# Linear attention into a softplus MLP on one core: x of tiles 9 to 11 turned by VectorE instead of TensorE, o of tiles 15 to 35 scaled by ScalarE head by head instead of by VectorE

## The chip, the cores and the metric

The kernel runs on one core of a Trainium2 chip. The core has TensorE (PE in the profile, with its weight loads as PEld), VectorE (DVE), ScalarE (ACT), GpSimd (POOL) and SyncE (SP, which here issues nearly all DMAs), each with its own in-order queue, an on-chip memory (SBUF) with 128 partitions, and PSUM, eight banks of 128 x 512 fp32 words into which TensorE accumulates. The metric is the device time of one launch in microseconds, lower is better.

## What is computed

The reference has two blocks, in fp32 precision. B, H, S, D are 8, 8, 576, 64.

```python
kv = np.einsum('bhsd,bhse->bhde', k, v)
out = np.einsum('bhsd,bhde->bhse', q, kv)
rms = np.sqrt(np.mean(out * out, axis=-1, keepdims=True) + 1e-06)
attn = out / rms * g_norm
x = attn.transpose(0, 2, 1, 3).reshape(4608, 512)
h = x @ w_in                       # 512 -> 2048
g = np.maximum(h, 0.0) + np.log1p(np.exp(-np.abs(h)))   # softplus
out = g @ w_out                    # 2048 -> 512
```

## The kernel before

**Tiles and blocks.** The 4608 tokens (batch times sequence) are 36 tiles of 128. Three tiles are a block (12 blocks of 384 tokens), four a wide block (9 of 512). `w_in` and `w_out` are cut into 16 chunks of 128 of the 2048 hidden units.

**Precision from three products.** TensorE multiplies a reduced-precision fp32 format (fp32r) at full rate. Each operand is kept as three pieces (a rounded high part, what it leaves, and a combination of both), and three matmuls with them make up one precise product. ScalarE writes the high piece, VectorE the other two. This split happens for x (`split`), for the weights (`split_weight`) and for softplus's output (`low`, `less`).

**Attention.** `kv_of(b)` loads k and v of a batch in five chunks each and sums k^T v in PSUM (L676); ScalarE copies the result out. `rows(t)` makes x of tile t:

- q is turned to q^T, for batches 0 and 1 by TensorE (`turn_q`, L756) with a ScalarE copy (L763), later by VectorE from blocks of 32 (L731, loads at L598);
- `out_rows` (L700) multiplies q^T by kv, 32 small matmuls, into a half of PSUM banks 2 and 3 (ring `o`, two places);
- ScalarE squares (L773), VectorE sums per head (`reduce`, L704), POOL takes the power -1/2 (`root`, L707 and L708), VectorE multiplies o by it (`norm`, L712) into x. `g_norm` is multiplied into `w_in` beforehand;
- x is turned to x^T. For tiles below `BY_PE` TensorE does it (`turn_x`, L718, four transposes); the first `AT_ONCE` = 6 tiles are split at once from PSUM; ScalarE copies x^T out of PSUM (L782) and SP stores it to DRAM (L783). For the other tiles VectorE transposes blocks of 32 x 32 in SBUF (`turn_blocks`, L799), and when the three tiles of a block are done SP stores them with four DMAs (L803), whose access pattern does the rest of the turn. It leaves the tokens of a block in another order, so the output rows of these tiles are put back in place by four DMAs per tile in the last pass (`leave`, L905) where others need one (L910).

From tile 6 on, x^T comes back from DRAM (`x_again`, L821) and is split (L620, L623, L626).

**MLP, first part.** 64 steps (`step`): blocks 0 to 3 go over hidden chunks 0 to 3, blocks 4 to 11 over chunks 0 to 5. A step is 12 matmuls of 384 columns for h (L843), softplus on ScalarE (L865), the split (L867, L854, L858) and 9 matmuls of 512 columns into the output sums (L850).

**MLP, second part.** The other chunks run over the wide blocks, 48 wide steps in two passes (`wide_step`, L1030 for h with a scheme that replaces eight products by seven, L1100 for the output). Partial sums go to DRAM between passes (`leave`, L895 and L910; `enter`, L889).

**Order.** The program order is written by a planner (`Plan.order`) before anything is emitted. Each piece of work is a task with an engine, a cost in ns, inputs, places it takes in rings of buffers, and a position `pos` in units of steps. The planner walks through its own clock: among the tasks of an engine that can start within 150 ns of the earliest, the lowest position goes first. `behind` ties a load to the first matmuls of a step: it may not be issued before them. Rows of tile t may not start before those of tile t - 1 (`follows`). From tile `BY_PE` + 1 on, an odd tile takes the position of the even tile before it and waits for both tiles' inputs, so that the two run together. Where TensorE would stand idle in the plan, a filler matmul of the identity is put in (`warm`, L1181); its result isn't used. Positions come from tables P0 to P7: `CONVERT` and `FETCH` (from P0) place the conversions and loads of the first eight weights, P4 the rows of the 36 tiles, P5 the kv and q of the batches, P7 the first k, v and q loads, P1 and P2 the later weights, P6 the units of x in the wide passes.

```python
        if n == 0: P4[t] + t * EARLY[0] + EARLY[1]
        else:      P4[t] + first_step["block", n] - (EARLY[2] if n == 1 else EARLY[3]) + t % TB * (len(CHUNKS[n]) // TB)
```

That is `x_pos(t)`, the position of tile t's rows, with `EARLY = P0[16:27]`.

Of the kernel before, what the change touches and what calls it, by code (L numbers as in the profile page):

```python
# [12 lines left out]
AF = mybir.ActivationFunctionType  # L13
# [42 lines left out]
class Plan:  # L56
# [20 lines left out]
        return Slot(ring)  # L77

    def add(self, engine, ns, run, after=(), pos=0.0, take=(), give=(), size=0, behind=None, follows=None, kind="all"):
        t = Task(engine, ns, run, [a for a in after if a is not None], pos, list(take), list(give), size)  # L80
        for s in t.give:
            s.readers += 1
        self.tasks.append(t)
        t.follows = follows
        t.behind = behind
        t.kind = kind
        return t
# [113 lines left out]
def kernel(  # L201
# [24 lines left out]
    nc = tc.nc  # L226
    B, H, S, D = q.shape
# [3 lines left out]
    NP = H // 2  # L231
# [14 lines left out]
    STEPS = [(ph, n, p) for ph in (1, 2) for n in range(n_wide) for p in PAIRS[ph - 1][n]]  # L246
    LAST = 2

    P0 = [-45.94, -26.77, -11.8, 0.28, -29.91, -5.64, -2.86, 3.84, -103.4, -98.98, -69.3, -76.66, -68.5, -24.67, -23.22, -34.97, 8.15, -43.02, 7.47, 9.69, 7.18, 18.16, -12.1, 4.75, 1.0, 95.98, -6.45, 6.38, 7.69, 5.17]
    P4 = [-30.17, -6.08, 16.93, -33.9, -22.35, -28.91, -17.33, -7.12, -9.75, -2.59, 0.87, 2.93, -12.14, -3.26, 0.98, 3.76, 7.8, -3.0, -2.25, 7.68, 20.89, 50.27, -0.5, -0.13, 26.66, 22.67, -11.61, -5.55, 2.74, 0.64, -0.48, 1.34, 0.64, 1.68, -8.4, -1.37]  # L250
    P5 = [1.24, -5.69, -2.28, 1.58, 5.58, 0.43, 5.83, -7.56, 3.01, -2.95, 3.18, 1.42, -14.52, 0.57, -1.29, -1.34]
    P6 = [-0.39, 4.6, -0.28, -2.24, -0.01, 1.05, 1.77, -3.9, -2.15, 0.85, 1.85, -1.74, 6.34, -2.44, -0.13, 3.82, 7.89, 0.51]
    P7 = [-23.78, -17.98, -11.85, -14.93, 0.41, 1.61, 7.35, 2.7, -25.02, -6.6, -15.2, -4.48, -2.14, 0.64, 2.93, 0.97, 4.67, 5.36, 3.33, 6.57, -10.37, 2.36, -14.11, -9.89, -7.11, 12.91, -2.89, 14.55, 12.59, 9.35]
    CONVERT, FETCH, EARLY, LATER = P0[:8], P0[8:16], P0[16:27], P0[27:]
    P1 = [48.8, 48.65, 66.31, 74.64, 125.35, 131.27, -11.31, 54.26, 67.75, 469.13, 282.82, 195.86]
    P2 = [22.14, 35.93, 25.02, 37.31, 52.38, 81.67, 74.61, 116.65, 106.27, 111.35, 100.82, -152.23, 99.52, 221.41, 428.54, -173.95, 119.58, -155.43, 317.87, 212.07, -7.69]
    P3 = [3.0, 2.86, 5.84, -16.31, 1.53, 3.03, 3.55, -20.64, 3.15, 2.55, 1.38, 1.52, 1.27, 0.75, 2.42, -1.39]
    SPLIT = {p: (P1[i], P1[6 + i]) for i, p in enumerate((2, 3, 4, 5, 6, 7))}
    TAKEN = {c: (P2[c - 6], P2[4 + c]) for c in range(6, 16)}
    LEAD, APART, AHEAD, MM2, LATE, SPLIT_G = P3[0], P3[1], P3[2], P3[3:11], P3[11:14], P3[14]  # L260
    EARLIER = P3[15]
    PACE = 2.5
    BY_PE = 12
    AT_ONCE = 2 * TB

    ctx.enter_context(tc.manual_schedule())
# [13 lines left out]
    scale = const.tile([P, 1], F32, name="scale")  # L280
# [4 lines left out]
    def space(name, words, late, dtype=F32):  # L285

        if (name, late) not in spaces:
# [13 lines left out]
                 h=2, o=2, tp=1, s0=1, s1=1, s2=1, s3=1, w=15, wh=3, u=4, u1=1, gvp=2, xl=2, ab=2)  # L301
# [9 lines left out]
    slot, add = plan.slot, plan.add  # L311
# [276 lines left out]
    def load_q(b):  # L588


        q_slots[b], q_loads[b] = slot("qa"), []
        pos = x_pos(first_tile[b] + 1) - EARLY[7] + P5[B + b]

# [93 lines left out]
    def rows(t):  # L687
        pos = x_pos(t)
        tp, qT, o, x, r, xp, xg = (slot(n) for n in ("tp", "n", "o", "x", "r", "tp" if t < AT_ONCE else "o", "n"))
# [36 lines left out]
        for b, r0, n, s0 in parts(t):  # L726
# [26 lines left out]
            def turn_q(n=n, q_s=q_s, at_qa=at_qa, tp=slot("tp" if t < AT_ONCE else "o")):  # L753
                y = new(tp, [P, NP, P])
                for p in range(NP):
# [4 lines left out]
                     behind=pos - 3.5, follows=first_load[0] if t and at_qa else None)  # L760
            first_load.append(ld)
            a = add("PE", 440, turn_q, [ld], pos - 1, [tp], [q_s])
# [6 lines left out]
        a = o_task = add("PE", 484, out_rows, turned + need, x_pos(t - second), [o], [qT], kind="rows", follows=rows_done.get(t - 1))  # L769
        rows_done[t] = a  # L770
        for pt in parts(t):
            o_tasks.setdefault(pt[0], []).append(a)
        a = add("ACT", 600, lambda: nc.scalar.activation(new(x, [P, H, D]).rearrange("s (a k) d -> s a (k d)", k=2), o.tile, func=AF.Square,  # L773
                                                              scale=D ** -0.5), [a], pos, [x])
        a = add("DVE", 690, reduce, [a], pos, [r])
        a = add("POOL", 2300, root, [a], pos)
        a = add("DVE", 700, norm, [a, o_task], pos, [], [o, r])
        if t < BY_PE:
            a = add("PE", 440, turn_x, [a], pos + 0.5, [xp], [x])
            if t < AT_ONCE:  # L780
                split(t, xp, a, pos + 0.5)
            a = add("ACT", 600, lambda: nc.scalar.copy(new(xg, [P, KD, P]), xp.tile), [a], pos + 1, [xg], [xp])  # L782
            x_there[t] = [add("SP", 450, lambda: nc.sync.dma_start(  # L783
                out=x_of(t), in_=xg.tile), [a], pos + 1, [], [xg], 1000)]
            return
# [3 lines left out]
        n, i = divmod(t, TB)  # L789
        g = TB if n < n_blocks - 1 else 1  # L790
        i0, i = i - i % g, i % g
        if i == 0:
            xb_slots[n] = slot("xb"), []
        xb, turns = xb_slots[n]
# [8 lines left out]
            nc.sync.dma_start(out=xd[n][:, i0 * P + a * g * BL:i0 * P + (a + 1) * g * BL].rearrange("(b i) m -> i b m", i=BL),  # L803
                              in_=xb.tile[a * BL:(a + 1) * BL].rearrange("i b t j -> i b (t j)"))

        turns.append(add("DVE", 710, turn_blocks, [a], pos, [] if i else [xb], [x], follows=turns[-1] if i else None))
        if i == g - 1:
            stores = [add("SP", 450, lambda a=a: store(a), turns, pos + 0.5, [], [xb], 820 if g > 1 else 490)
                      for a in range(P // BL)]
# [339 lines left out]
    for c in range(KF):  # L1149
        for j in (2 * c, 2 * c + 1):  # L1150
            if c < OWN:
                pos = CONVERT[j] if c < 4 else LATER[c - 4] + LATER[2] * (j % 2)
                weight(j, pos, FETCH[j] if c < 4 else pos, pos - 3.5)
            else:
                fetch, pos = (x + P2[20] * (j % 2) for x in TAKEN[c])
# [61 lines left out]
```

## Time and profile before

| | |
|---|---|
| median of 4 runs | 873.57 us (872.46 to 874.26) |
| the profiled execution | 874.26 us |
| its span, first to last instruction | 872.5 us |
| granted TensorE clock | 0.999 |
| TensorE matmuls, busy | 855.4 us, 98% |
| TensorE weight loads, busy | 758.3 us, 87% |
| VectorE busy | 703.9 us, 81%, 992 instructions |
| ScalarE busy | 521.8 us, 60%, 979 instructions |
| POOL busy | 78.2 us, 9% |
| DMA | 167.07 MB, 191 GB/s in the mean |

In the views below, a row of groups has the line, engine, operation, output and input tiles by the program's names, shapes, count, then busy us and mean ns of one, then the idle time of its engine just before it and what ended it. A row of waits has engine and line that waited, what it waited for, us in total, times, and the longest. Busy TensorE doesn't mean TensorE at its peak rate, and a wait for several things is put down to the one that came last.

### The profile page before, as it was taken

The page shows a single profiled execution, that of the slowest core. Times are in us where ns is not written, and L with a number is a line of the kernel's source. Part 1 is how long each engine was busy: PE and PEld are TensorE (multiplying, and loading weights), DVE is VectorE, ACT ScalarE, POOL GpSimd, SP SyncE. Part 2 cuts the span into 40 slices and gives each one's busy share as a digit, 9 for nine tenths or more (in the row PEclk, how much of TensorE's full clock was granted, in tenths as well). Part 3 has the DMA queues.
Part 4 walks back from the last instruction along what each step waited for, and adds up shares of the span by engine and source line. Part 5 has one row for each costly group of instructions (what it writes and reads, how often), then busy time and mean ns, then how long its engine had stood idle before and what let it go on. Part 6 is the DMA issues. An engine that isn't in the chain of part 4 may idle for free.

```text
span 872.5 us, 17016 instructions
## 1 busy us (share of the span) xinstructions
PE 855.4 (98%) x6464; PEld 758.3 (87%) x6464; DVE 703.9 (81%) x992; ACT 521.8 (60%) x979; POOL 78.2 (9%) x79
## 2 busy tenths in 40 slices
PE   7799999999999999999999999999999999999998
PEld 5578888989898899989988998888899899999986
DVE  7888888978788788798988779877788766878873
ACT  5766654545444567766757556655777555566653
POOL 0352223121112300000000000000000000000000
PEclk9999999999999999999999999999999999999999
DMA  9999999898993765427554545655364753777764
GB/s 265 283 224 221 269 219 251 171 276 211 219 169 104 176 194 174 149 85 250 181 156 147 181 156 187 201 157 180 110 195 135 238 160 107 244 222 237 236 187 130
DMA packets 239634, 167.07 MB, mean 191 GB/s; under 512 B 106304, under 2 KB 198464, under 8 KB 239552
## 3 DMA queue, kind: packets, MB, share of 16 engines
q1 hardware_dynamic: 239392, 165.99, 68.6%
q8 instruction: 50, 0.82, 0.4%
q14 instruction: 32, 0.26, 0.1%
q10 hardware_dynamic: 160, 0.00, 0.0%
HBM read 112.98 MB, written 52.95 MB: 190 GB/s over the span
## 4 chain that ended last, share of the span: by engine, by line
PE 89%; DMA 4%; DVE 2%; SPq 2%; ACT 1%; issue 1%; POOL 0%; DVEq 0%; POOLq 0%; ACTq 0%
PE banks L1100 30%; PE banks L1030 27%; PE banks L850 13%; PE banks L843 13%; PE banks L700 2%; PE banks L676 2%; DMA early<-in_q_dram 2%; SPq L598 1%; DMA loads<-in_v_dram 1%; DMA x<-w 1%; DMA loads<-in_k_dram 1%; SPq L665 1%; DVE units L623 0%; PE banks L1181 0%; DVE half L712 0%
## 5 line engine op out<-in xcount | busy, mean ns | idle before, releaser
L1100 PE MATMUL banks<-pieces,gv 128*128 128x512 f32 x696 | 217.9, 394 | 0.0
L843 PE MATMUL banks<-units,pieces 128*128 128x384 f32 x768 | 145.8, 338 | 0.0
L850 PE MATMUL banks<-pieces,gv 128*128 128x512 f32 x576 | 145.5, 396 | 0.0
L843 PEld LDWEIGHTS banks<-units,pieces 128*128 128x128 f32 x768 | 135.1, 188 | 5.1
L1100 PEld LDWEIGHTS banks<-pieces,gv 128*128 128x128 f32 x696 | 121.2, 189 | 18.1
L1100 PE MATMUL banks<-pieces,g_False 128*128 128x512 f32 x348 | 136.4, 392 | 0.1
L1030 PEld LDWEIGHTS banks<-units,pieces 128*128 128x128 f32 x948 | 126.9, 190 | 8.3 <-ACT banks L1075 1.3
L1030 PE MATMUL banks<-units,pieces 128*128 128x256 f32 x948 | 132.5, 282 | 0.0
L850 PEld LDWEIGHTS banks<-pieces,gv 128*128 128x128 f32 x576 | 106.3, 188 | 20.9
L1090 DVE TENSOR_TENSOR gv<-g_True,gv 128x1024 fp32r<-128x1024 f32 x48 | 58.7, 1224 | 34.0 <-ACT gv L1087 34.0
L865 ACT ACTIVATE half<-banks 128x384 f32<-128x384 f32 x64 | 31.4, 490 | 89.1 <-PE banks L843 88.9
L1100 PEld LDWEIGHTS banks<-pieces,g_False 128*128 128x128 f32 x348 | 65.4, 188 | 15.4 <-DVE g_False L1093 0.6
L708 POOL TENSOR_TENSOR r<-r,half 128x8 f32<-128x8 f32 x36 | 63.2, 1756 | 3.0
L1079 DVE TENSOR_TENSOR g_True<-banks,g_True 128x512 f32<-128x512 f32 x48 | 33.2, 691 | 37.3 <-PE banks L1030 33.3
L1057 ACT ACTIVATE g_True<-banks 128x256 f32<-128x256 f32 x96 | 36.8, 383 | 39.7 <-PE banks L1030 39.2
L1093 DVE SCALAR_TENSOR_TENSOR g_False<-gv 128x1024 fp32r<-128x1024 f32 x48 | 58.7, 1223 | 1.3
L993 DVE TENSOR_TENSOR units<-loads,units 128x1024 fp32r<-128x1024 f32 x42 | 51.2, 1219 | 8.7 <-ACT units L990 8.7
L1030 PEld LDWEIGHTS banks<-units,w 128*128 128x128 f32 x396 | 52.5, 189 | 2.8
L1030 PE MATMUL banks<-units,w 128*128 128x256 f32 x396 | 54.8, 281 | 0.0
L990 ACT ACTIVATE units<-loads 128x1024 fp32r<-128x1024 f32 x42 | 44.5, 1058 | 17.0 <-PE banks L1030 11.0
L996 DVE SCALAR_TENSOR_TENSOR units<-units 128x1024 fp32r<-128x1024 f32 x42 | 51.3, 1223 | 1.6
L1087 ACT ACTIVATE gv<-g_True 128x1024 fp32r<-128x1024 f32 x48 | 51.0, 1061 | 1.5
(116 smaller groups left out, 1295.4 us busy)
## 6 DMA issues: line engine op xcount, KB each, us to landing
loads<-x SPq DMA_DIRECT2D x180, 128.0 KB, 2.8
part<-m SPq DMA_DIRECT2D x72, 256.0 KB, 2.8
m<-part SPq DMA_DIRECT2D x72, 256.0 KB, 3.5
loads<-form SPq DMA_DIRECT2D x45, 256.0 KB, 3.3
form<-loads SPq DMA_DIRECT2D x36, 256.0 KB, 2.7
raw<-in_moe_w_in_dram SPq DMA_DIRECT2D x16, 512.0 KB, 4.6
loads<-in_k_dram SPq DMA_DIRECT2D x32, 256.0 KB, 4.5
loads<-in_v_dram SPq DMA_DIRECT2D x32, 256.0 KB, 4.8
```

What stands on the lines that cost most here:

```text
L708: nc.gpsimd.tensor_tensor(out=r.tile, in0=r.tile, in1=half, op=ALU.pow)
L843: nc.tensor.matmul(hp, lhsT=w_in.tile[:, i, kd * P:(kd + 1) * P], rhs=xv.tile[:, i, kd], start=(m == 0), stop=(m == 3 * KD - 1))
L850: nc.tensor.matmul(mine[i].tile, lhsT=gv.tile[:, m, i * P:(i + 1) * P], rhs=w_out.tile[:, m], start=(c == cs[0] and m == 0), stop=(c == cs ...
L990: nc.scalar.activation(part_of(0, F32R), xl.tile if m > 1 else xl.tile[:, 0], func=AF.Copy, scale=DOWN)
L993: nc.vector.tensor_tensor(out=part_of(1, F32R), in0=xl.tile if m > 1 else xl.tile[:, 0], in1=part_of(0), op=ALU.subtract)
L996: nc.vector.scalar_tensor_tensor(out=part_of(2, F32R), in0=part_of(1), scalar=-RADIX, in1=part_of(0), op0=ALU.mult, op1=ALU.add)
L1030: nc.tensor.matmul(place(q), lhsT=w[:, m, at:at + P], rhs=dst.tile[:, m, v, kd] if u < 6 else dst.tile[:, m, kd], start=(u == 0 and not m ...
L1057: nc.scalar.activation(dst, src, func=AF.Softplus, scale=1.0 + E)
L1087: nc.scalar.activation(gvt(0, F32R), gt(), func=AF.Copy, scale=DOWN)
L1090: nc.vector.tensor_tensor(out=gvt(1, F32R), in0=gt(), in1=gvt(0), op=ALU.subtract)
L1093: nc.vector.scalar_tensor_tensor(out=gt(F32R), in0=gvt(1), scalar=-RADIX, in1=gvt(0), op0=ALU.mult, op1=ALU.add)
L1100: nc.tensor.matmul(mine[i].tile, lhsT=(gvt(m, F32R) if m < 2 else gt(F32R))[:, c, i * P:(i + 1) * P], rhs=outs[c].tile[:, m], start=fresh ...
```

## The change

`BY_PE` goes from 12 to 9: x of tiles 9, 10 and 11 takes VectorE's path (`turn_blocks`, one block of three tiles) instead of `turn_x`, ScalarE's copy and three stores. As `BY_PE` is also used in `second` and in `leave`, tiles 10 and 11 now run together, and the output rows of tiles 9 to 11 are stored with four DMAs per tile.

A new constant `BY_ACT` = 15: from tile 15 on, the multiplication of o by the per-head factor is done by ScalarE, in two tasks of four instructions (`norm_half`), each on the 64 columns of one head with the head's factor as a per-partition scale, in place of one VectorE instruction for all eight heads.

All tables P0 to P7 get other numbers, and positions are rounded to four places.

```diff
--- before.py
+++ after.py
@@ -77,6 +77,7 @@
         return Slot(ring)
 
     def add(self, engine, ns, run, after=(), pos=0.0, take=(), give=(), size=0, behind=None, follows=None, kind="all"):
+        pos, behind = round(pos, 4), None if behind is None else round(behind, 4)
         t = Task(engine, ns, run, [a for a in after if a is not None], pos, list(take), list(give), size)
         for s in t.give:
             s.readers += 1
@@ -246,21 +247,22 @@
     STEPS = [(ph, n, p) for ph in (1, 2) for n in range(n_wide) for p in PAIRS[ph - 1][n]]
     LAST = 2
 
-    P0 = [-45.94, -26.77, -11.8, 0.28, -29.91, -5.64, -2.86, 3.84, -103.4, -98.98, -69.3, -76.66, -68.5, -24.67, -23.22, -34.97, 8.15, -43.02, 7.47, 9.69, 7.18, 18.16, -12.1, 4.75, 1.0, 95.98, -6.45, 6.38, 7.69, 5.17]
-    P4 = [-30.17, -6.08, 16.93, -33.9, -22.35, -28.91, -17.33, -7.12, -9.75, -2.59, 0.87, 2.93, -12.14, -3.26, 0.98, 3.76, 7.8, -3.0, -2.25, 7.68, 20.89, 50.27, -0.5, -0.13, 26.66, 22.67, -11.61, -5.55, 2.74, 0.64, -0.48, 1.34, 0.64, 1.68, -8.4, -1.37]
-    P5 = [1.24, -5.69, -2.28, 1.58, 5.58, 0.43, 5.83, -7.56, 3.01, -2.95, 3.18, 1.42, -14.52, 0.57, -1.29, -1.34]
-    P6 = [-0.39, 4.6, -0.28, -2.24, -0.01, 1.05, 1.77, -3.9, -2.15, 0.85, 1.85, -1.74, 6.34, -2.44, -0.13, 3.82, 7.89, 0.51]
-    P7 = [-23.78, -17.98, -11.85, -14.93, 0.41, 1.61, 7.35, 2.7, -25.02, -6.6, -15.2, -4.48, -2.14, 0.64, 2.93, 0.97, 4.67, 5.36, 3.33, 6.57, -10.37, 2.36, -14.11, -9.89, -7.11, 12.91, -2.89, 14.55, 12.59, 9.35]
+    P0 = [-51.25, -13.31, -28.11, -0.89, -52.51, -4.9, -19.5, 4.49, -140.62, -126.44, -88.51, -96.46, -100.38, -25.43, -13.98, -42.06, -28.49, -36.42, 39.41, 8.82, 7.23, 22.63, -4.14, 5.1, 0.41, 111.95, -26.5, 7.48, 7.3, 9.79]
+    P4 = [-49.82, -17.44, 59.53, -31.74, -18.17, -38.56, -25.79, -19.7, -34.43, 4.73, -0.03, 1.95, -28.04, -3.12, 0.5, 25.22, 41.05, -18.71, -5.41, -2.55, 39.47, 59.13, -19.46, -5.64, 37.83, -4.77, -24.21, -8.59, 4.34, 26.33, -70.4, 7.18, -0.45, 18.64, -3.13, -7.41]
+    P5 = [15.74, 2.22, -4.87, 7.5, 6.25, 15.53, 4.47, -15.68, -3.43, 32.09, 1.42, -2.23, -6.68, 3.2, -5.1, -0.0]
+    P6 = [-5.0, 0.89, -7.05, -17.85, -7.47, -3.43, 4.32, -4.14, -3.37, 0.93, -0.84, -12.54, 1.35, 1.5, 2.03, 6.96, -6.46, 4.89]
+    P7 = [-37.82, -42.49, -14.06, -16.33, 3.68, 6.23, -8.09, 6.34, -35.36, -15.84, -14.25, -22.01, -0.93, 0.05, 24.27, 24.25, 1.0, 14.93, 4.27, 14.15, -7.88, 6.08, -27.64, -8.35, -2.32, 37.25, -1.33, 16.45, 19.25, 23.37]
     CONVERT, FETCH, EARLY, LATER = P0[:8], P0[8:16], P0[16:27], P0[27:]
-    P1 = [48.8, 48.65, 66.31, 74.64, 125.35, 131.27, -11.31, 54.26, 67.75, 469.13, 282.82, 195.86]
-    P2 = [22.14, 35.93, 25.02, 37.31, 52.38, 81.67, 74.61, 116.65, 106.27, 111.35, 100.82, -152.23, 99.52, 221.41, 428.54, -173.95, 119.58, -155.43, 317.87, 212.07, -7.69]
-    P3 = [3.0, 2.86, 5.84, -16.31, 1.53, 3.03, 3.55, -20.64, 3.15, 2.55, 1.38, 1.52, 1.27, 0.75, 2.42, -1.39]
+    P1 = [52.19, 51.92, 57.77, 61.84, 111.12, 131.27, 23.25, 58.31, 66.8, 507.77, 251.61, 203.48]
+    P2 = [23.31, 35.62, 27.15, 38.1, 47.95, 82.07, 69.55, 100.38, 112.9, 104.49, 277.58, -87.75, 236.15, 134.35, 481.42, -149.3, 298.33, -275.07, 382.49, 222.8, -6.08]
+    P3 = [1.73, 2.69, 5.92, -7.65, 1.34, 2.39, 4.99, -16.33, 3.25, 3.38, 3.17, 1.76, 1.0, -5.76, 0.17, -3.08]
     SPLIT = {p: (P1[i], P1[6 + i]) for i, p in enumerate((2, 3, 4, 5, 6, 7))}
     TAKEN = {c: (P2[c - 6], P2[4 + c]) for c in range(6, 16)}
     LEAD, APART, AHEAD, MM2, LATE, SPLIT_G = P3[0], P3[1], P3[2], P3[3:11], P3[11:14], P3[14]
     EARLIER = P3[15]
     PACE = 2.5
-    BY_PE = 12
+    BY_PE = 9
+    BY_ACT = 15
     AT_ONCE = 2 * TB
 
     ctx.enter_context(tc.manual_schedule())
@@ -774,9 +776,17 @@
                                                               scale=D ** -0.5), [a], pos, [x])
         a = add("DVE", 690, reduce, [a], pos, [r])
         a = add("POOL", 2300, root, [a], pos)
-        a = add("DVE", 700, norm, [a, o_task], pos, [], [o, r])
+        def norm_half(e):
+            for h in range(e * NP, e * NP + NP):
+                nc.scalar.activation(x.tile[:, h], o.tile[:, h // 2, h % 2 * D:h % 2 * D + D], func=AF.Identity,
+                                     scale=r.tile[:, h:h + 1])
+
+        if t < BY_ACT:
+            a = [add("DVE", 700, norm, [a, o_task], pos, [], [o, r])]
+        else:
+            a = [add("ACT", 900, lambda e=e: norm_half(e), [a, o_task], pos, [], [o, r]) for e in range(2)]
         if t < BY_PE:
-            a = add("PE", 440, turn_x, [a], pos + 0.5, [xp], [x])
+            a = add("PE", 440, turn_x, a, pos + 0.5, [xp], [x])
             if t < AT_ONCE:
                 split(t, xp, a, pos + 0.5)
             a = add("ACT", 600, lambda: nc.scalar.copy(new(xg, [P, KD, P]), xp.tile), [a], pos + 1, [xg], [xp])
@@ -803,7 +813,7 @@
             nc.sync.dma_start(out=xd[n][:, i0 * P + a * g * BL:i0 * P + (a + 1) * g * BL].rearrange("(b i) m -> i b m", i=BL),
                               in_=xb.tile[a * BL:(a + 1) * BL].rearrange("i b t j -> i b (t j)"))
 
-        turns.append(add("DVE", 710, turn_blocks, [a], pos, [] if i else [xb], [x], follows=turns[-1] if i else None))
+        turns.append(add("DVE", 710, turn_blocks, a, pos, [] if i else [xb], [x], follows=turns[-1] if i else None))
         if i == g - 1:
             stores = [add("SP", 450, lambda a=a: store(a), turns, pos + 0.5, [], [xb], 820 if g > 1 else 490)
                       for a in range(P // BL)]
```

## The prediction

> **What bounds the kernel now.** I read the page's busy shares first, then the chain that ended last, then busy time by stage, then TensorE's waits stage by stage.
>
> ```profile
> PE 855.4 (98%) x6464; PEld 758.3 (87%) x6464; DVE 703.9 (81%) x992; ACT 521.8 (60%) x979; POOL 78.2 (9%) x79
> PE 89%; DMA 4%; DVE 2%; SPq 2%; ACT 1%; issue 1%; POOL 0%; DVEq 0%; POOLq 0%; ACTq 0%
> ```
>
> TensorE (PE) is busy 98% of 872.5 us and carries 89% of the chain. What is left, DMA above all, lies in the first part of the chain. The stages say where TensorE has room (columns: stretch, its length, busy time of PE, PEld, DVE, ACT, POOL, granted clock, DMA share, GB/s):
>
> ```profile
> 40.00:50.00 10.00, 8.93 (x159) 7.31 (x155) 8.51 (x15) 6.03 (x12) 4.12 (x4) 1.00 1.04 238
> 70.00:82.70 12.70, 12.59 (x199) 10.40 (x196) 10.73 (x20) 8.98 (x19) 3.88 (x4) 1.00 1.00 178
> 82.70:123.00 40.30, 38.67 (x406) 33.94 (x404) 35.74 (x61) 23.96 (x47) 10.61 (x10) 1.00 0.99 230
> 123.00:308.00 185.00, 185.00 (x1715) 165.13 (x1712) 154.82 (x266) 89.25 (x177) 43.03 (x41) 1.00 0.85 203
> 363.20:868.60 505.40, 505.26 (x3159) 454.07 (x3157) 397.81 (x466) 313.11 (x572) 0.00 (x0) 1.00 0.57 179
> ```
>
> From 123 us to 868.6 us TensorE doesn't stop. The 48 wide steps fill the last 505.4 us at 10.53 us each (42 matmuls of 256 columns, 24 of 512). Time can be won there only by taking TensorE work away. Between 82.7 and 868 us TensorE's waits consist of one line, and from 61 us on of two:
>
> ```profile
> PE banks L676 <- DMA loads<-in_v_dram: 1.6, 1, 1.6
> PE banks L718 <- DVE half L712: 0.5, 1, 0.5
> ```
>
> Before 82.7 us the stretches add up to 11.4 us of idle TensorE, and all of the fillers (L1181, matmuls whose result nobody reads, issued by the plan where it has nothing else) are there:
>
> ```profile
> L1181 PE MATMUL banks<-ident_r 128*128 128x512 f32 x52 | 18.8, 480 | 2.0 <-DVE ident_r L1141 1.6 <-ACT pieces L509 0.2
> ```
>
> So 30.2 us of the first 82.7 are without useful TensorE work; 8.9 of them pass before the first k and v have landed at 8.88 us, and 21.3 depend on the order of loads and of the first tiles. From 10 us on DMA's share is about 1 there, and DVE is busy 81 to 95%.
>
> **The change part by part.** Rows that price it:
>
> ```profile
> L712 DVE TENSOR_TENSOR half<-banks,r 128x512 f32<-128x512 f32 x36 | 24.7, 687 | 6.7 <-PE banks L700 4.1 <-POOL r L708 2.4
> L799 DVE STREAM_TRANSPOSE turned<-half 128x512 f32<-128x512 f32 x24 | 16.7, 704 | 0.5
> L782 ACT COPY w<-banks 128x512 f32<-128x512 f32 x12 | 7.0, 587 | 4.4 <-PE banks L718 4.4
> L895 ACT ACTIVATE m<-banks,scale 128x512 f32<-128x512 f32 x36 | 24.6, 688 | 15.7 <-PE banks L1100 15.7
> L895 ACT ACTIVATE m<-banks 128x512 f32<-128x512 f32 x72 | 41.7, 594 | 11.9 <-PE banks L1100 6.7 <-PE banks L850 2.3 <-DVE m L444 1.4
> L1071 ACT COPY banks<-banks 128x256 f32<-128x256 f32 x48 | 17.4, 362 | 6.4 <-PE banks L1030 6.3
> ```
>
> Tiles 9 to 11. TensorE loses three groups of four transposes (L718). In the timeline the groups at 80.12, 82.71 and 93.63 us push the next matmul back by 0.42, 0.35 and 0.36 us: 1.1 us of TensorE, in a part where it has no other gap, so I count it in full. ScalarE loses 3 x 0.587 = 1.8 us (L782), VectorE gains 3 x 0.704 = 2.1 us (L799), at 90% busy. Three stores of 256 KB (median 4.8 us to landing) become four of 192 KB (4.0 us), which can only start when the third tile is turned; SP issues one more. These tiles' output stores in the last pass become four DMAs each instead of one: nine more on SP, at 0.42 us 3.8 us, hidden by SP's waits there (the pass's stores and loads wait for ACT and DVE for tens of us). Without that cover, the loads queued behind them (L940) would be late by up to 1.3 us per tile. Tile 11 now shares its place with 10 instead of standing alone, at most one switch, 0.1 us: taken as nothing.
>
> Tiles 15 to 35. VectorE loses 21 x 0.687 = 14.4 us, mostly in 123 to 308 us, where it falls from 84% to about 77%. TensorE waits for it there nowhere, so that is worth nothing by itself. ScalarE gets 168 instructions of 64 columns with a per-row scale, of a shape the trace doesn't show. Row: (587 - 362) / 256 = 0.88 ns a column gives 362 - 192 x 0.88 = 193 ns, and a scale from a tile adds 688 - 594 = 94: 287 ns. Two equal instructions in a row (L773) took 1.09 us instead of 1.19, so some 0.10 us overlaps. Four then take 0.85 us, and 1.15 without overlap; I take 0.9, near the lower end, since back-to-back work of this engine overlaps wherever the timeline shows it. 42 x 0.9 = 38 us (36 to 48) more on ScalarE, which goes from 48% to about 69% in that stretch. A tile's x comes 2 x 0.9 - 0.69 = 1.1 us later, and its part of the o bank is free 1.1 us later; both are hidden as long as the next pair of tiles is some 16 us away, as it is between the L700 groups at 145.64, 161.07 and 185.41 us. If that cover is gone, the next out_rows stands behind a bank for up to 1.1 us a tile.
>
> The Trainium skill, page "ScalarE: Activation LUTs", section "Rules for kernel authors", speaks against this part: multiplies belong on VectorE. From the same page's section "What ACT_TABLE_LOAD costs" one would estimate 186 + 53 + 93 = 332 ns for one such instruction, 93 of them overlapped, 1.05 us for four, and 44 us in all in place of 38; its 93 ns for a scale by pointer agrees with the 94 of the rows. The rule looks at the cost of the instruction; this trace has the idle time on ScalarE to pay for it, and no wait of TensorE that VectorE's shorter list would shorten.
>
> The order. All position tables change. They don't add work, but decide what the first 82.7 us look like. Two effects can be priced. Rows of tile 2, the last tile that step 0 needs, stand at -33.9 instead of -9.8 and so sixth instead of seventh among the tiles; tiles follow each other there by (42.29 - 28.18) / 3 = 4.7 us (starts of L718): up to 4.7 us won. Against that, the last k or v chunk of batch 0 has one more weight (512 KB) and one more q tile (256 KB) in front of it: 768 KB at the 283 to 293 GB/s of 10 to 40 us is 2.7 us lost. Between -4.7 and +2.7 I take -2.0: the chain into the first L843 at 45.85 goes through a tile's split (L623 at 40.31), not through batch 0's loads, whose last lands at 26.4. The wait of 1.6 us at 121.74 is for a v chunk of batch 4; its load goes from position 26.6 to 16.9 and may start one step earlier, its matmuls 1.7 steps earlier. Ends: -1.6 and 0; I take -1.6, as the priority of the load moves much further than the matmul.
>
> Sum against the profiled execution (874.26 us, span 872.5 and 1.8 around it): -1.1 - 1.6 - 2.0 = -4.7, 869.6 us. That execution lies 0.7 above the median of the four; 873.57 - 4.7 = 868.9, so 869.0.
>
> **The rivals.**
>
> *ScalarE's new work holds up softplus (slower).* In a steady step L843 ends at 179.2, softplus (L865) starts at 179.23, L858 ends at 181.53 and its L850 starts at 183.22: 1.6 us of slack. One half (0.9) in front of softplus fits. Two in a row (1.7 to 2.3) don't, and lose 0.1 to 0.7 us; it decides from 1.6 us of foreign work ahead of one softplus. At 21 tiles x 0.4 this is 8.4, less the 1.1 of the transposes: 881 us. For it: ScalarE works in order, and POOL's root (1.66 us) releases both halves at once. Against it: the work is put in as two halves that something may go between, and the ScalarE row shows 87 us of waiting ahead of L865, 1.7 us at a time.
>
> *Block 3's x comes late (slower).* Tile 9's rows go from -0.3 to 7.9, and 10 and 11 may not start before it, so all three may run only with step 8. Tile 14, which already takes this path, needed 28.2 us from its rows (111.87) to its block's first L843 (140.07); step 8 to 12 is 117.23 - 95.46 = 21.8 us. TensorE then stands up to 6.4 us, 877 to 879 us. For it: in the trace the third split of block 3 ends at 117.53, with step 12 starting at 117.23, so there is nothing to spare. Against it: any idle moment of TensorE lets these rows in earlier, and the 21.3 us say there are many.
>
> *It comes to nothing.* The new order wins 1 us in the head and loses it elsewhere: 872.5.
>
> *The head gains more.* A third of the 21.3 us, an estimate: 7 instead of 2, 864 us.
>
> **How the numbers follow.** Runs of this kernel lie within 0.2% of each other, which is about what can be told from no change: 1.75 us. Forecast 0.43 (866 to 871.8), more from the head 0.12 (858 to 866), nothing 0.14 (871.8 to 875.3), block 3 late 0.15 (875.3 to 880), ScalarE in front of softplus 0.16 (876 to 888). Faster 0.55, same 0.14, slower 0.31. The range 861.5 to 881 leaves out about 0.05 below and 0.1 above; the likeliest case alone has 866 to 871.8. Most of the width is the order of the first 82 us, which rows of the old order price badly.
>
> **What would show it.** TensorE's total on L718 down by a quarter to 36 instructions, L782 at 9, L799 at 27. A ScalarE group of 168 with 64 columns, 0.2 to 0.34 us each, and 15 instructions of VectorE's norm (L712's line) instead of 36. L1030 and L1100 still filling 505 us. The first L843 before 45.7 us, fewer fillers and under 30 us lost before the saturated part. No wait for v at about 120 us. Wrong would be: TensorE waits for ScalarE or VectorE in 123 to 308 us (first rival), a TensorE gap just before the 13th group of L843 (second), or a first L843 clearly later than 45.7 us.

## The result, and the profile after

The changed kernel takes 876.19 us (median of 52 runs, 873.33 to 880.75), the kernel before 874.02 us (78 runs) beside it. The ratio is 1.0025, 95% interval 1.0017 to 1.0033: slower by 2.2 us, where 4.7 us less was forecast. In the profiled executions the span is 875.1 us against 872.5.

Busy time and the chain on the page of after:

```profile
PE 858.0 (98%) x6447; PEld 759.6 (87%) x6447; DVE 693.4 (79%) x974; ACT 554.7 (63%) x1144; POOL 81.0 (9%) x79
PE 87%; DMA 5%; SPq 3%; DVE 2%; ACT 1%; issue 1%; POOL 0%; DVEq 0%; ACTq 0%
```

TensorE is idle for 875.1 - 858.0 = 17.1 us. Before it was 872.5 - 855.4 = 17.1 as well. The 2.6 us are therefore *busy* time of TensorE, though it has twelve transposes and five fillers less to do. Of the chain, DMA and SP's queue have 8% instead of 6%.

The groups that the edits touch (columns as in the groups shown before):

```profile
L781 ACT ACTIVATE half<-banks,r 128x64 f32<-128x64 f32 x168 | 37.2, 327 | 6.9 <-POOL r L710 6.8
L714 DVE TENSOR_TENSOR half<-banks,r 128x512 f32<-128x512 f32 x15 | 10.3, 686 | 3.2 <-PE banks L702 2.2 <-POOL r L710 0.7
L809 DVE STREAM_TRANSPOSE turned<-half 128x512 f32<-128x512 f32 x27 | 18.9, 704 | 1.4 <-ACT half L781 1.2
L720 PE MATMUL banks<-ident_r,half 128*128 128x128 f32 x36 | 6.2, 301 | 1.2 <-DVE half L714 1.2
L702 PE MATMUL banks<-early,w 64*64 64x64 f32 x1152 | 23.5, 227 | 1.6 <-ACT w L765 0.7 <-ACT half L781 0.5 <-DVE half L714 0.4
```

All counts are those of the edits: 168 small instructions of ScalarE, 15 norms, 27 turns by VectorE, 36 transposes. But the transposes of the remaining tiles take 301 ns each, and the 1152 small matmuls of out_rows (L702, L700 before) 23.5 us, where the kernel before spent 22.0 on the same 1152. That is the first sign of where busy time came from. The stages (columns as before):

```profile
82.70:123.00 40.30, 40.30 (x452) 35.43 (x454) 34.76 (x59) 22.02 (x43) 12.42 (x11) 1.00 1.03 227
123.00:308.00 185.00, 184.22 (x1732) 163.53 (x1725) 146.43 (x253) 123.77 (x350) 46.64 (x42) 1.00 0.84 210
363.20:868.60 505.40, 505.19 (x3162) 453.68 (x3161) 400.01 (x469) 314.32 (x573) 0.00 (x0) 1.00 0.58 179
```

From 82.7 us on TensorE hardly stops, at a granted clock of 1.00, and its waits there are two:

```profile
PE banks L702 <- ACT half L781: 0.5, 1, 0.5
PE banks L678 <- DMA loads<-in_v_dram: 0.3, 1, 0.3
```

So what was lost was lost before 82.7 us. Short stretches of the head (the part up to there) show it; the third number from the end, ahead of DMA's share and GB/s, is the granted clock:

```profile
25.00:27.00 2.00, 1.24 (x9) 0.97 (x10) 1.29 (x3) 1.50 (x4) 0.89 (x2) 1.00 1.04 301
27.00:29.00 2.00, 0.54 (x4) 0.23 (x2) 1.97 (x4) 2.00 (x6) 1.83 (x3) 1.00 0.97 234
29.00:32.00 3.00, 2.56 (x53) 2.16 (x53) 2.06 (x4) 1.24 (x3) 1.59 (x1) 0.76 1.22 193
32.00:34.00 2.00, 1.82 (x27) 1.51 (x22) 1.29 (x2) 0.26 (x2) 0.00 (x0) 0.50 0.79 200
34.00:36.00 2.00, 2.00 (x29) 1.35 (x31) 0.31 (x1) 1.07 (x2) 0.00 (x0) 0.50 1.00 328
36.00:40.00 4.00, 3.25 (x31) 2.04 (x23) 3.18 (x6) 3.47 (x7) 1.98 (x2) 0.83 1.05 280
```

After a gap near 27.5 us TensorE is granted half its clock, from about 30.5 to 37.4 us. The kernel before has 1.00 in each of these stretches; two of them:

```profile
29.00:32.00 3.00, 2.53 (x28) 1.66 (x26) 2.74 (x5) 2.71 (x7) 0.18 (x1) 1.00 1.12 313
32.00:34.00 2.00, 1.91 (x69) 1.63 (x69) 1.91 (x4) 2.00 (x5) 0.00 (x0) 1.00 1.12 349
```

What the missing clock costs, as an estimate from these rows (busy time by one minus the clock): 2.56 x 0.24 + 1.82 x 0.50 + 2.00 x 0.50 + 3.25 x 0.17 = 3.1 us. TensorE's timeline (start, length, group, idle before and its releaser) has the gap and what follows:

```profile
27.06 0.47 PE L1191 MATMUL banks<-ident_r 128*128 128x512 f32 x1
29.44 0.69 PE L678 MATMUL banks<-loads 128*64 128x64 f32 x16 [1.90 <-DMA loads<-in_k_dram]
31.07 1.13 PE L702 MATMUL banks<-early,w 64*64 64x64 f32 x32
33.43 1.12 PE L720 MATMUL banks<-ident_r,half 128*128 128x128 f32 x4
47.51 2.70 PE L853 MATMUL banks<-units,pieces 128*128 128x384 f32 x14
```

A k chunk of batch 1 is waited for during 1.90 us; no filler stands there, since the planner puts fillers only where TensorE is idle by its own clock, and by that it was not. Then 32 small matmuls take 1.13 us and four transposes 1.12, where the same groups take 0.69 and 0.66 us at full clock. The first step starts at 47.51 us instead of 45.69. The kernel before has a gap too, a shorter one, and keeps its clock behind it:

```profile
26.53 0.69 PE L676 MATMUL banks<-loads 128*64 128x64 f32 x16 [1.35 <-DMA loads<-in_v_dram]
45.69 2.27 PE L843 MATMUL banks<-units,pieces 128*128 128x384 f32 x12
```

Loads run later in the new order: in the first 36 us they move 247 GB/s, 8.89 MB, where the kernel before moved 279 GB/s, 10.04 MB. By 82.7 us TensorE has done 7 matmuls of L853, 32 of kv and 32 of rows less than before, 1.23 + 1.24 + 0.62 = 3.1 us of work; before 82.7 it was idle for 12.4 us instead of 11.4.

### The profile page after: what moved, and what is told of

It reads as the page before. It is cut to its first block, busy times and chain, and to the rows that moved or that the text cites. A ratio compares the mean times of both kernels' runs of the same rounds, so it can differ in the third digit from the quotient of the medians.

```text
span 875.1 us, 17137 instructions
## 1 busy us (share of the span) xinstructions
PE 858.0 (98%) x6447; PEld 759.6 (87%) x6447; DVE 693.4 (79%) x974; ACT 554.7 (63%) x1144; POOL 81.0 (9%) x79
## 4 chain that ended last, share of the span: by engine, by line
PE 87%; DMA 5%; SPq 3%; DVE 2%; ACT 1%; issue 1%; POOL 0%; DVEq 0%; ACTq 0%
PE banks L1110 30%; PE banks L1040 27%; PE banks L853 13%; PE banks L860 12%; DMA loads<-in_v_dram 2%; PE banks L678 2%; SPq L600 2%; PE banks L702 2%; DMA m<-x 1%; DMA g<-in_moe_w_out_dram 1%; SPq L667 1%; DMA loads<-in_k_dram 1%; PE banks L1191 1%; DVE half L714 0%; DMA early<-in_q_dram 0%
## 5 line engine op out<-in xcount | busy, mean ns | idle before, releaser
L1110 PE MATMUL banks<-pieces,gv 128*128 128x512 f32 x768 | 240.8, 395 | 0.0
L1110 PE MATMUL banks<-pieces,g_False 128*128 128x512 f32 x384 | 150.4, 392 | 0.1
L860 PE MATMUL banks<-pieces,gv 128*128 128x512 f32 x576 | 145.7, 397 | 0.0
L1110 PEld LDWEIGHTS banks<-pieces,gv 128*128 128x128 f32 x768 | 130.4, 189 | 15.8
L853 PE MATMUL banks<-units,pieces 128*128 128x384 f32 x768 | 144.0, 337 | 0.0
L853 PEld LDWEIGHTS banks<-units,pieces 128*128 128x128 f32 x768 | 135.2, 188 | 4.7
L860 PEld LDWEIGHTS banks<-pieces,gv 128*128 128x128 f32 x576 | 106.2, 187 | 21.6 <-DVE gv L868 0.4
L1040 PEld LDWEIGHTS banks<-units,pieces 128*128 128x128 f32 x840 | 112.5, 190 | 7.8 <-ACT banks L1085 0.6
L1040 PE MATMUL banks<-units,pieces 128*128 128x256 f32 x840 | 116.1, 282 | 0.0
L1110 PEld LDWEIGHTS banks<-pieces,g_False 128*128 128x128 f32 x384 | 72.1, 188 | 17.1 <-DVE g_False L1103 0.6
L1040 PEld LDWEIGHTS banks<-units,w 128*128 128x128 f32 x504 | 67.5, 189 | 5.5 <-ACT banks L1085 0.9
L1040 PE MATMUL banks<-units,w 128*128 128x256 f32 x504 | 69.7, 281 | 0.0
L710 POOL TENSOR_TENSOR r<-r,half 128x8 f32<-128x8 f32 x36 | 66.2, 1839 | 3.0
L864 DVE TENSOR_TENSOR gv<-half,gv 128x384 fp32r<-128x384 f32 x64 | 35.3, 552 | 29.1 <-ACT gv L877 27.7
```

Source lines behind the costliest of these rows:

```text
L710: nc.gpsimd.tensor_tensor(out=r.tile, in0=r.tile, in1=half, op=ALU.pow)
L853: nc.tensor.matmul(hp, lhsT=w_in.tile[:, i, kd * P:(kd + 1) * P], rhs=xv.tile[:, i, kd], start=(m == 0), stop=(m == 3 * KD - 1))
L860: nc.tensor.matmul(mine[i].tile, lhsT=gv.tile[:, m, i * P:(i + 1) * P], rhs=w_out.tile[:, m], start=(c == cs[0] and m == 0), stop=(c == cs ...
L864: nc.vector.tensor_tensor(out=gv.tile[:, 1], in0=g.tile, in1=gv.tile.bitcast(F32)[:, 0], op=ALU.subtract)
L1040: nc.tensor.matmul(place(q), lhsT=w[:, m, at:at + P], rhs=dst.tile[:, m, v, kd] if u < 6 else dst.tile[:, m, kd], start=(u == 0 and not m ...
L1110: nc.tensor.matmul(mine[i].tile, lhsT=(gvt(m, F32R) if m < 2 else gt(F32R))[:, c, i * P:(i + 1) * P], rhs=outs[c].tile[:, m], start=fresh ...
```

## The experiments

My theory after the comparison: the two edits are nearly free where they lie, and the head of the new order costs the time, by the late k chunk and the half clock behind it. Rivals: ScalarE's new work costs it by holding up softplus (the first rival); the turn by VectorE costs it (the second); differences of the clock from run to run.

### The parts by themselves, planned anew

Four kernels take the change apart by its constants and tables, each ordered anew by the planner.

The new tables without the two edits (against after):

```diff
-    BY_PE = 9
-    BY_ACT = 15
+    BY_PE = 12
+    BY_ACT = 36
```

> All new position tables, but x of tiles 9 to 11 turned by TensorE and o scaled by VectorE, as before. Theory 'head' (the new order of the first 83 us costs some 3 us: TensorE waits for batch 1's k and v, and its clock falls to half at 31 to 37 us): the loss stays and the 1.1 us of the transposes come on top, 876.5 to 878 against some 874. Rival 'ScalarE' (the new work on ScalarE and its splitting of rows into singles costs the time): back to 873 to 874.5.

Measured: 893.20 us (891.88 to 895.17), ratio 1.0211 (1.0188 to 1.0233). Waits of TensorE behind 50 us:

```profile
PE banks L702 <- ACT half L775: 3.8, 2, 3.4
PE banks L702 <- DVE half L714: 3.0, 2, 2.5
```

Both edits, with the tables that place the first loads, conversions, rows, kv and q as before (against after, lists shortened):

```diff
-    P0 = [-51.25, -13.31, -28.11, -0.89, -52.51, -4.9, -19.5, 4.49, -140.62, ...
+    P0 = [-45.94, -26.77, -11.8, 0.28, -29.91, -5.64, -2.86, 3.84, -103.4, ...
...
```

(P4, P5 and P7 likewise.)

> Both edits, with the tables that place phase 0 (P0, P4, P5, P7) of before and the tables of the later weights and of the wide passes (P1, P2, P3, P6) of after. Head: the half clock and the waits at 27 to 33 us are gone, 872.5 to 873.5, at or below before. ScalarE: 875.5 or more, as after.

Measured: 895.76 us, ratio 1.0257 (1.0232 to 1.0281). The largest wait is that of out_rows for ScalarE's new work. It is the wait for a place in the o bank that the prediction names as hidden, not softplus:

```profile
PE banks L702 <- ACT half L781: 4.3, 3, 2.8
```

The kernel before with the other new tables, P1, P2, P3 and P6 (against before, shortened):

```diff
-    P1 = [48.8, 48.65, 66.31, 74.64, 125.35, 131.27, -11.31, 54.26, 67.75, ...
+    P1 = [52.19, 51.92, 57.77, 61.84, 111.12, 131.27, 23.25, 58.31, 66.8, ...
...
```

> Before, with only the tables of the later weights and the wide passes (P1, P2, P3, P6) of after, neither edit. Head: 873.5 to 874.5, nothing to gain or lose there, as TensorE is never idle in that part. The difference of this run to the one with both edits and the same tables is the price of the edits: -1.1 us by the prediction's sum, +1 to +2 by ScalarE.

Measured: 888.25 us, ratio 1.0157 (1.0135 to 1.0179). One wait is 3.5 us long:

```profile
PE banks L700 <- DVE half L712: 3.5, 1, 3.5
```

The turn of tiles 9 to 11 alone, with all tables of before (against after, shortened; P1 to P7 likewise):

```diff
-    BY_ACT = 15
+    BY_ACT = 36
...
-    P0 = [-51.25, -13.31, -28.11, -0.89, -52.51, -4.9, -19.5, 4.49, -140.62, ...
+    P0 = [-45.94, -26.77, -11.8, 0.28, -29.91, -5.64, -2.86, 3.84, -103.4, ...
...
```

> Only x of tiles 9 to 11 turned by VectorE, all tables of before, o still scaled by VectorE. The prediction's sum: -1.1 us for 12 transposes, 872.5 to 873.3. Its second rival (block 3's x late): 876 to 879, with a gap of TensorE before the 13th group of L853.

Measured: 882.92 us, ratio 1.0093 (1.0071 to 1.0115). Waits, behind 50 us:

```profile
PE banks L853 <- ACT units L622: 2.8, 1, 2.8
PE banks L853 <- DVE units L625: 1.9, 1, 1.9
```

What follows: every mixture loses 8 to 21 us, far outside all that was expected, with waits each in another place, and the sum of the parts is nowhere near the whole (2.2 us). The parts can't be priced this way, since a new plan moves everything; tables and edits belong together. The last one shows x coming late, but not in block 3: its two waits end at 97.16 and 175.13 us, in the 9th and the 23rd group of L853, the first ones of blocks 2 and 5. The 13th, block 3's first, starts at 121.44 us without a wait. There is no run of ScalarE's edit alone, or of both edits together, planned anew with all of before's tables.

So the other experiments keep a program order as it is, and change only what is issued at a place in it.

### The order of after, with o scaled by VectorE again

One VectorE instruction takes the place of the first task of four; the second issues nothing. What is left out of the change is ScalarE's work alone.

```diff
-            a = [add("ACT", 900, lambda e=e: norm_half(e), [a, o_task], pos, [], [o, r]) for e in range(2)]
+            a = [add("ACT", 900, lambda e=e: None if e else norm(), [a, o_task], pos, [], [o, r]) for e in range(2)]
```

> The program order of after, untouched, but o of tiles 15 to 35 is scaled by one VectorE instruction, put where the first ScalarE half stood; the second half is left out. Theory 'head' (all of the loss lies in the first 83 us, ScalarE's work is hidden): within 0.7 us of after, 875.5 to 877 against some 874.3 for before. Rival 'ScalarE' (168 small instructions get into the way of softplus): 873 to 874.5, and TensorE's 0.8 us of waits at 123 to 211 us gone.

Measured: 876.88 us (876.0 to 878.16), ratio 1.0036 (1.0023 to 1.0048), no faster than after's 1.0025. TensorE's waits behind 83 us:

```profile
PE banks L860 <- DVE gv L864: 0.9, 1, 0.9
PE banks L860 <- DVE gv L868: 0.2, 1, 0.2
```

The 0.5 us behind ScalarE's scaling are gone, and 1.1 us behind VectorE's split of softplus stand in their place. In the order of after, ScalarE's 37 us cost nothing that six runs can show, and VectorE in its place holds TensorE up by as much. The first rival falls for this order.

### The order of before, with o scaled by ScalarE

```diff
-        a = add("DVE", 700, norm, [a, o_task], pos, [], [o, r])
+        def by_heads():
+            for h in range(H):
+                nc.scalar.activation(x.tile[:, h], o.tile[:, h // 2, h % 2 * D:h % 2 * D + D], func=AF.Identity,
+                                     scale=r.tile[:, h:h + 1])
+
+        a = add("DVE", 700, norm if t < 15 else by_heads, [a, o_task], pos, [], [o, r])
```

> The program order of before, untouched, but o of tiles 15 to 35 is scaled by eight ScalarE instructions in place of the one of VectorE. Hidden work, as predicted: within 0.7 us of before. ScalarE in front of softplus (the prediction's first rival, eight in one piece here): +2 to +8 us, with waits of TensorE for VectorE's split at 123 to 308 us.

Measured: 876.62 us (9 runs), ratio 1.003 (1.0017 to 1.0044). The same work that is free in the order of after costs in this one, where eight instructions come in one piece and no place was kept for them. Held against before, matmul by matmul, the profiled execution (878.10 us) is 1.42 us late at 121.7 us, ahead of the part with the changed instructions, 3.72 at 305 us and 3.83 at the end: 2.3 us lie in 123 to 305. Half of that, from 2.26 to 3.43 us late, comes behind 170.65 us, where eight of the small instructions (1.74 us, from 170.70) stand between a softplus and its split and eight more (1.80 us, from 172.68) ahead of the next softplus. That is the first rival's mechanism. TensorE's waits behind 50 us name only a part:

```profile
PE banks L676 <- DMA loads<-in_v_dram: 1.1, 2, 0.9
PE banks L855 <- DVE gv L859: 0.3, 1, 0.3
PE banks L855 <- DVE gv L863: 0.2, 1, 0.2
```

The first 1.42 us have nothing to do with the edit, which isn't there yet. They are from a v chunk that landed 0.67 us later in this execution, and the half clock behind it:

```profile
40.39 0.69 PE L676 MATMUL banks<-loads 128*64 128x64 f32 x16 [1.25 <-DMA loads<-in_v_dram]
42.36 1.07 PE L756 MATMUL banks<-ident_r,w 128*128 128x128 f32 x4 [0.56 <-DMA w<-in_q_dram]
43.35 1.13 PE L700 MATMUL banks<-early,w 64*64 64x64 f32 x32
44.42 1.12 PE L718 MATMUL banks<-ident_r,half 128*128 128x128 f32 x4
```

Two gaps, 1.25 and 0.56 us, and the rows and transposes behind them have 1.13 and 1.12 us, as in after. That pointed to the clock.

### The gaps of after filled

Seven more fillers, 1.8 us of them, behind the 32nd, where the gap of 1.90 us is; in the first version also five near 7 us. They don't bring the late chunk earlier: TensorE still has nothing useful to do until it lands. What they can change is the clock behind the gap.

```diff
-    plan.spare = ("h", warm, 400, mm1s[6][1])
+    more, count = {7: 5, 32: 7}, [0]
+
+    def warm_on(s):
+        warm(s)
+        count[0] += 1
+        for _ in range(more.get(count[0], 0)):
+            nc.tensor.matmul(s.tile, lhsT=ident_r, rhs=ident_r.unsqueeze(1).to_broadcast([P, 4, P]), start=True, stop=True)
+
+    plan.spare = ("h", warm_on, 400, mm1s[6][1])
```

> After, with five more filler matmuls in TensorE's gap at 5 to 7.5 us and seven more in its gap at 27.5 to 29.4 us; nothing else. Theory 'clock' (idle gaps of 2 us in the ramp are followed by several us at half clock): no 0.5 clock at 31 to 37 us, mean clock nearer to 1 and 1.5 to 2.5 us less than after, 873.5 to 874.7. Rival 'loads' (TensorE stands behind batch 1's k and v, the clock doesn't matter): as after, 876.

Measured: 874.80 us (12 runs), ratio 1.0006 (0.9994 to 1.0019). Then the second gap alone (`more = {32: 7}`):

> The changed kernel with seven more fillers after its 32nd alone, that is in the gap of TensorE near 27.5 us, and none in the gap near 7 us. Theory (the gap near 27.5 us, 1.90 us long, and the half clock behind it cost the head about 2 us): the granted clock stays above 0.9 from 28 to 36 us, the first group of L853 starts near 45 us instead of 47.51, and the median lies at 874.5 to 875.3, with the version that filled both gaps. Rival (the gain of that version came from the early gap, or from run to run): the first step may start earlier, but the median stays with the changed kernel's, 876 to 876.8.

Measured: 874.44 us (12 runs; before, beside it, 875.36), ratio 1.0000 (0.9985 to 1.0016). Windows and timeline of this second version:

```profile
27.00:29.00 2.00, 2.00 (x12) 1.37 (x10) 1.97 (x4) 2.00 (x6) 1.83 (x3) 1.00 0.99 245
29.00:32.00 3.00, 3.00 (x73) 2.48 (x73) 2.71 (x6) 1.40 (x4) 1.54 (x1) 1.00 1.27 220
32.00:34.00 2.00, 1.84 (x38) 1.09 (x36) 1.08 (x2) 1.59 (x4) 0.00 (x0) 1.00 0.95 273
34.00:36.00 2.00, 1.79 (x9) 1.18 (x9) 1.97 (x4) 2.00 (x5) 0.44 (x1) 1.00 1.02 299
```

```profile
27.27 1.78 PE L1200 MATMUL banks<-ident_r 128*128 128x512 f32 x7
28.99 0.69 PE L678 MATMUL banks<-loads 128*64 128x64 f32 x16
44.77 5.47 PE L853 MATMUL banks<-units,pieces 128*128 128x384 f32 x29
```

The clock stays at 1.00, and the first step starts at 44.77 us, 2.7 earlier, on 1.8 us of work that nobody reads. The chunk's matmuls (L678) start at 28.99 us instead of 29.44, so at most 0.45 of the 2.7 can be its landing; the rest is the clock. The early gap is not needed for it. Taken together, the 36 runs of the three versions with the gap filled (a third follows) average 874.94 us, the 71 runs of after (53 with a recorded clock, one more than above) and of the two kernels with its head and no more fillers 876.46: 1.5 us for the half clock. Pairs that ran side by side give rather more in their medians: 876.88 and 874.80 us, 876.56 and 874.14. It is less than the 2.7 by which the head came earlier, in part since a v chunk is waited for longer behind it (0.8 us in this version, 0.3 in after), a wait that earlier matmuls run into.

The new head isn't better than the old one even so. The first step starts 0.92 us earlier than in before, but by 82.7 us TensorE has done 32 matmuls of kv less and only three of L860 more, and the launch takes as long as before's.

### The same gap opened in before

```diff
-    plan.spare = ("h", warm, 400, mm1s[6][1])
+    count = [0]
+
+    def warm_or_not(s):
+        count[0] += 1
+        if not 30 <= count[0] <= 45:
+            warm(s)
+
+    plan.spare = ("h", warm_or_not, 400, mm1s[6][1])
```

> Before, with fillers 30 to 45 (of 52, those between 23 and 45 us) left out; they compute nothing that is used. Clock: gaps of 1 to 2 us open, the clock falls in the ramp, +1 to +3 us. Loads: no effect, within 0.7 us of before.

Measured: 873.19 us (12 runs), ratio 0.9991 (0.9981 to 1.0000): not slower at all.

```profile
27.00:29.00 2.00, 1.53 (x19) 1.38 (x20) 1.99 (x4) 0.79 (x2) 1.83 (x3) 0.50 1.12 286
29.00:32.00 3.00, 2.82 (x12) 2.12 (x12) 2.32 (x4) 2.30 (x5) 0.63 (x1) 0.50 1.03 305
32.00:34.00 2.00, 2.00 (x43) 1.55 (x46) 1.97 (x5) 1.33 (x3) 0.00 (x0) 0.59 1.08 322
```

The half clock is there, from 27 to about 33 us, and puts TensorE 1.5 us behind in 32 to 40 us, but the first step only by 0.43 (46.12 for 45.69). The 16 fillers had kept room of their own, and slow work took it up. Later the v wait at 121.74 is gone, since its chunk has landed when TensorE comes to it, and the last matmul is 1.46 us earlier than in before. So a half clock costs little where the stretch has slack.

### The output products brought forward

In after the first output product (L860) starts at 64.71 us, in before at 59.86. Here the split of steps 0 and 1 stands earlier on VectorE, and six products take the places of fillers 41 to 46.

```diff
+    done = plan.order()
...
+    places = [next(t for t in dve if t.start >= at) for at in (48500, 52700)]
+    for k in range(2):
+        for t in first_splits[k]:
+            done.remove(t)
+            done.insert(done.index(places[k]), t)
+    for k in range(6):
+        done.remove(first_outs[k])
+        done[done.index(fillers[40 + k])] = first_outs[k]
```

> The program order of after, with one stretch rearranged by hand: VectorE's split of the first two steps (L864, L868), which stood at 62.5 to 65.2 us behind work on x, is put where it stood in the plan's order at 48.5 and 52.7 us, and the six output products of these steps (L860) take the places of the six fillers between 52 and 62 us. Theory 'order' (in 54 to 64.7 us TensorE has no matmul of the MLP to run because VectorE's queue holds the split back): 1.5 to 2.5 us less than after, 873.7 to 874.7. Rival 'x first' (the work on x that is pushed back by 2.2 us of VectorE sets the end): as after, 876 to 877.

Measured: 876.56 us (12 runs), ratio 1.0018 (1.0004 to 1.0032), against after's 1.0025. Step 3 starts at 66.87 instead of 69.32 us, but three transposes now wait, and a v chunk:

```profile
PE banks L720 <- DVE units L625: 1.0, 1, 1.0
PE banks L720 <- DVE half L714: 0.9, 1, 0.9
PE banks L720 <- ACT w L792: 0.8, 1, 0.8
PE banks L678 <- DMA loads<-in_v_dram: 0.7, 1, 0.7
```

With the fillers of the gap version as well:

> The same rearrangement and, with it, the fillers in TensorE's gaps at 5 and 27.5 us, which alone had brought after from 876.2 to 874.8. Order and clock add up: 872 to 873.3, below before (874.0). If both remove the same wait: 874 to 874.8.

Measured: 874.14 us (12 runs), ratio 1.0008 (0.9992 to 1.0023). That is what the fillers win alone; the rearrangement adds nothing that can be told. Its profiled execution is one of the two slowest of the 12 (878.49 us), and one late load makes most of that:

```profile
PE banks L678 <- DMA loads<-in_v_dram: 2.8, 1, 2.8
```

### Before with a later head

Seven fillers, 1.5 us, stand ahead of the first L843.

```diff
+        for _ in range(7 if count[0] == 48 else 0):
+            nc.tensor.matmul(s.tile, lhsT=ident_r, rhs=ident_r.unsqueeze(1).to_broadcast([P, 4, P]), start=True, stop=True)
```

> Before, with seven more fillers (1.5 us) ahead of the first L843. If the wait of 1.6 us for v at 121.7 us is slack that such a delay only fills, as the run with dropped fillers suggests: 874 to 874.6, and no wait for v at 120 us. If every delay of the ramp goes through to the end: 875.3 to 875.8.

Measured: 875.15 us (12 runs; before, beside it, 874.20), ratio 1.0014 (0.9999 to 1.0029). This lies between the two expectations, nearer to the delay that goes through. In the profiled execution (874.59 us), held against before matmul by matmul, TensorE is 1.2 us late up to 119 us and 0.43 from 122 us to the end: the wait for v has 0.8 us instead of 1.6.

```profile
PE banks L676 <- DMA loads<-in_v_dram: 0.8, 1, 0.8
```

So what a head that is earlier or later is worth at the end differs: 1.5 of 2.7 us with the gap filled; here 0.43 of 1.2 in the profiled execution, but some 1.2 by the ratio. Where it is less than the whole, a wait for a later batch's load takes up the difference. None of the kernels beats before by more than can be measured.

## Why the prediction was wrong

**The order: the head, -2.0 us taken, between -4.7 and +2.7.** This is the step that failed, in sign. I argued that the chain into the first L843 goes through a tile's split and not through the loads, from the old order alone, and so took the side of tile 2. The runs show the other end, and a term that the step did not have, the granted clock: fewer bytes moved in the first 36 us (247 for 279 GB/s, and still only 253 with the gap filled, so the order does it and not the clock), a k chunk of batch 1 that TensorE comes to 1.90 us too early, and behind that a half clock that costs some 3.1 us of busy time, an estimate. The first L853 came at 47.51 us, which the prediction had named as its sign of error. That the half clock costs 1.5 us of the 2.2 is shown by the versions with fillers. But the forecast gain isn't there at full clock either: with the clock kept, the first step comes 0.92 us earlier than in before, and none of that is left at 82.7 us. That the order of the loads makes the chunk late is argued from the bytes; no run moved it alone. What the remaining 0.7 us are is open: their interval (ratio 1.0000, 0.9985 to 1.0016, in the last one) takes in zero. The late output products were a candidate, and moving them forward won nothing that can be told.

**The wait for v at 121.74 us, -1.6 us.** Gone as forecast (0.3 us is left, at 175.7). But the time did not follow from it in full: 0.5 us went into a wait for ScalarE at 144.5 us, and the length of the chunk's wait depends on when TensorE comes to it as well as on the load. A late TensorE makes it shorter without a gain, as the version with a later head shows (1.6 to 0.8 us there).

**Three groups of transposes, -1.1 us counted in full.** The instructions are gone (36 for 48), and TensorE's busy time in L720 fell by 1.3 us (7.5 to 6.2), in spite of the half clock. Counting them in full was wrong in part: two of the three groups lay at 80.12 and 82.71 us, in a stretch whose length the loads and the clock set in after. Only the third, 0.36 us, lay where TensorE is saturated.

**ScalarE's price, 0.9 us for four (0.85 to 1.15).** Right: eight take 1.74 us in the timeline, 0.87 for four, and 37.2 us in all for 38 forecast.

```profile
142.72 1.74 ACT L781 ACTIVATE half<-banks,r 128x64 f32<-128x64 f32 x8 [0.43 <-POOL r L710]
```

The Trainium skill's page "ScalarE: Activation LUTs" (section "What ACT_TABLE_LOAD costs") gives the figures by which four were estimated at 1.05 us; for these instructions that is too high, and the measured 0.87 decides.

**ScalarE's work is hidden, VectorE's relief is worth nothing.** Right in this order, as the version of after with VectorE's norm shows. ScalarE is busy 123.77 of the 185 us, 67% for 69% forecast; VectorE 79% instead of 77. Slack is a property of the order, not of the engine: in before's order the same instructions cost 2.3 us in the profiled execution.

**The rivals.** ScalarE in front of softplus: one wait of 0.5 us in after, for a place in the o bank, and not 8.4; its mechanism is real elsewhere, in the order of before. (The slack of 1.6 us that it starts from is 183.22 - 181.53 = 1.7.) Block 3's x late: TensorE is busy for all of 82.7 to 123 us, so no; the same edit, planned anew with before's tables, has such waits (2.8 and 1.9 us for the units of L853), but in blocks 2 and 5. "It comes to nothing" and "the head gains more" both had a gain in the head, and there was a loss. The time itself lies near that of "block 3's x comes late", by coincidence, with nothing of its mechanism.

**Fewer fillers, under 30 us lost.** 47 fillers for 52, as forecast, but 19.4 us in them for 18.8 (520 ns each for 480); one that stands alone in the half clock, at 36.40 us, takes 0.79 us. With 12.4 us of idle time in front of 82.7 us that makes 31.8, not under 30. Counting fillers says little when the clock is another.

## What to carry to other kernels

Price a change of order at its worst place: where TensorE stands a microsecond or two for a load in the ramp, the price can be that gap and a half clock for the next microseconds. Filler work in the gap saves the half clock, not the gap. Edits to a planned program are priced in the order that they come with; moving one part into another order costs more than the edit itself. Work for an idle engine was free here only in the order that kept a place for it.

## What the runs showed of the hardware

A gap as short as 1.90 us was followed by a granted clock of 0.50 for some 6.8 us. In before's order with fillers left out, TensorE was busy for only 0.51 of the 2 us from 25 to 27, and the clock was 0.50 from 27 to 32. The length of one gap doesn't tell it alone: the gaps of 1.25 and 0.56 us together were enough in the order of before with ScalarE's scaling, while before's single gap of 1.35 us was not. The busy time of the 3.4 us in which they lie tells these apart: 1.51 us in after (27.15 to 30.56), 1.57 in the run with the two gaps (38.97 to 42.38), 1.01 with fillers left out (23.39 to 26.80), each with a half clock straight behind; 2.06 in before (24.78 to 28.19), without one. It gives no sharp limit: 1.81 us had a half clock behind it in before with the later tables (23.81 to 27.22), 1.71 none in before with fillers left out (37.03 to 40.45). The Trainium skill, page "TensorE: Matmul & The Clock Gate", section "HAM oscillation — how this bites in real kernels", gives idle gaps of more than about 3.4 us as those to avoid. Shorter ones were enough here.

The mean granted clock of an execution goes with its time. Of the 53 executions of after with a recorded clock, the 12 at 0.9985 or more took 874.5 us in the mean, the 17 at 0.9945 or less 878.3. Of 84 of before that ran beside the experiments, the 10 at 0.9985 or more took 873.5 us and the 9 at 0.9945 or less 876.5; where their clock fell is not known. With the gap filled, none of 36 executions was at 0.9945 or less. In before with its fillers left out, 8 of 12 were, and they took 873.7 us: the same low clock, in a stretch with room for it.
